# Two output-projection loads a layer: the last two columns moved by 114 and 14 partitions

## The chip, the cores and the metric

The kernel runs on one core of one Trainium2 chip. The metric is device time in microseconds (us) for one execution. Before the change three runs gave 518.45, 520.19 and 518.1 us, median 518.45.

## What is computed

One token passes through two identical layers. Each layer is an attention block A and a mixing MLP block B, both with a residual:

```python
def _A_ref(x, k_cache, v_cache, wq, wo):
    W = min(4096, max(256, Sk // 4))                  # 4096 positions
    q = (x @ wq) per head                             # 32 heads of 192
    k, v = the last W positions of each head's cache
    p = softmax(q k^T * 192 ** -0.5)
    return (p v, all heads side by side) @ wo         # (6144,) @ (6144, 640)

x = x + _A_ref(_layernorm(x), A_k_cache, A_v_cache, A_wq, A_wo)
x = x + _B_ref(_layernorm(x), B_w1, B_w2, B_w3, B_w4)
x = x + _A_ref(_layernorm(x), ...)                    # same weights and caches again
x = x + _B_ref(_layernorm(x), ...)
```

With one position, B's first half falls away (its shifted parts are zero), so B is a layernorm, `w3` (640 x 1536), a gelu and `w4` (1536 x 640). Everything is bf16 in memory. A head's window of K, or of V, is 1.5 MB; they and the weights make the 216 MB that the kernel reads. Layer 1 finds seven transposed K windows and part of the V windows still in SBUF from layer 0.

## The kernel before

**Memory.** One SBUF tensor, `cells`, is cut into eleven cells of 12,288 bytes a partition, each large enough for one head's K or V window. A table, `home`, written out by hand, says which cell each piece uses. `take` claims a cell and `give` frees it in program order; a load into a cell waits until the last reader of the cell's former content is done.

**Loads.** All loads are issued by SP, on one queue, in the fixed order of the list `stream`, and each is called when some later piece of work needs it (`need`). The heads go in groups of four. For each group SP issues K of the next group and V of this one alternately, mostly two heads at a time (`load_both`, line 159: 128 partitions of 24,576 bytes), and then, with one group's delay, the 768 rows of `wo` that belong to the group (`load_wo`, lines 193 to 201: 128 partitions of 7,680 bytes, six rows of `wo` on each partition, "columns" c of 640 values below). Layer 0 takes the groups from the last to the first, layer 1 from the first to the last. So `wo` piece (layer 0, c = 4) is the fourth `wo` load of the kernel, and (0, 2) the sixth; (1, 3) and (1, 5) are the third and fifth of layer 1. The last two `wo` loads of layer 1 are already cut into (3, 3) and (3, 2, 1) columns. At a layer's end come `w3` (`load_w3`, lines 209 and 211) and `w4` (`load_w4`, lines 224 to 229).

**Semaphores.** Each transfer tells of its landing on one of eight semaphores, taken in turn; a transfer whose semaphore was used before waits on SP until the transfer eight places earlier has landed.

**Work on the data.** DVE transposes each K quarter (line 422), PE computes scores (line 501), the softmax steps go over DVE, ACT and PE (lines 530 to 598), PE multiplies with V (line 630), and the group's result is folded (`o_fold`) and multiplied with `wo`: in `out_row` (line 679) for the middle groups and `out_proj` (line 661) or line 701 for the others. `out_row` for a group runs while the next group's softmax is under way. The mixer multiplies with `w3` at line 990 and with `w4` at line 1037, each after the landing of its last piece; layer 1 of attention needs the mixer's result.

The first transfers are five loads of `wq` and, behind the first of them, `load_x` (line 146), which fills five partitions of 256 bytes. At the end the result leaves in the same form from line 1061.

Of the kernel before, what the change touches and what calls it, by code (L numbers as in the profile page):

```python
# [16 lines left out]
P = 128  # L17
# [17 lines left out]
def kernel(  # L35
# [14 lines left out]
    nc = tc.nc  # L50
    _, _, D = A_x.shape
# [22 lines left out]
    NA = Dh // 32  # L74
    NKX = 6
    NKEEP, NCELL = 7, 11
    WARM = 4

# [54 lines left out]
    def take(key):  # L135
        i = cell_of[key] = home[key]
        free.remove(i)
        return cell(i)
# [54 lines left out]
    def load_wo(layer, c):  # L193
        t = take(("wo", layer, c))
        src = A_wo[c * QC:(c + 1) * QC, :].rearrange("(p c) n -> p (c n)", c=NA)
        parts = {NG - 2: (3, 3), NG - 1: (3, 2, 1)}.get(c, (NA,)) if layer == 1 else (NA,)
        i = 0
        for n in parts:
            nc.sync.dma_start(t[:, i * D:(i + n) * D], src[:, i * D:(i + n) * D])
            i += n  # L200
        return t

# [12 lines left out]
    def load_w4(layer):  # L215
# [17 lines left out]
        return blocks  # L233

    LOADERS = {"x": load_x, "k": load_k, "v": load_v, "wq": load_wq, "wo": load_wo, "w3": load_w3, "w4": load_w4}

    def layer_stream(layer):
# [115 lines left out]
    warm_ps = psm.tile([32, 32], F32, tag="psm")  # L353
    for i in range(WARM):
        nc.tensor.matmul(warm_ps[:], lhsT=Eq[:, 0, :], rhs=Eq[:, 0, :], start=(i == 0), stop=(i == WARM - 1))

# [735 lines left out]
```

## Time and profile before

| quantity | value |
|---|---|
| median of three runs | 518.45 us |
| the profiled execution's own time | 518.16 us |
| its span, first to last instruction | 516.4 us |
| read from memory | 216.47 MB, 419 GB/s over the span |
| packets of SP's queue (q1) | 17,572, with 98.6% of the time of 16 DMA engines |
| busy: PE, DVE, ACT | 62%, 55%, 9% of the span |
| `wo` loads of 960 KB | 13, median 28.2 us from issue to landing |

The shares of busy time are averages over the whole span. The DMA share counts the time that packets took on the 16 DMA engines of the core. The trace also keeps a record of each packet (its start, length, size and queue, but not its engine) and of each landing: a 128-partition transfer adds one to its semaphore sixteen times, once for each engine that carried a part of it, and has landed with the sixteenth.

### The profile page before, as it was taken

What the parts mean: (1) busy time and instruction counts of PE and PEld (TensorE: products, weight loads), DVE (VectorE), ACT (ScalarE), POOL (GpSimd) and SP (SyncE); (2) the same over time, 40 slices, a digit from 0 to 9 for tenths busy, and PEclk for the clock granted to TensorE, in tenths of its full rate; (3) what the DMA queues carried; (4) which work ended last, traced back from release to release, by engine and by line L of the source; (5) the groups of instructions that cost most, each with busy time, mean ns of one, the idle gap of its engine ahead of it and who ended that gap; (6) DMA issues with size and microseconds to landing.
All of it is one profiled execution on the core that took longest, in us unless ns stands there. A gap on an engine that the chain in (4) does not pass through costs nothing. (4 is left out here: it accounts for less than half of the span.)

```text
span 516.4 us, 9514 instructions
## 1 busy us (share of the span) xinstructions
PE 318.0 (62%) x4132; PEld 197.3 (38%) x4132; DVE 285.2 (55%) x642; ACT 48.6 (9%) x173; POOL 4.0 (1%) x16
## 2 busy tenths in 40 slices
PE   1046775745386666867645975767474674546775
PEld 0024343423244333544423643444243352323444
DVE  2056668647456565665714256766555764635722
ACT  1000102010010101010101011010010100100011
POOL 2000000000000000000000000000000000000000
PEclk9999998777756567675655588675758677865665
DMA  8999999999999999999999999999999999999995
GB/s 343 438 436 428 429 430 428 435 430 421 440 430 433 428 428 438 420 424 429 428 424 394 384 427 425 441 426 435 428 426 436 428 435 430 425 435 434 424 411 232
DMA packets 17613, 217.07 MB, mean 420 GB/s; under 512 B 1828, under 2 KB 2340, under 8 KB 7972
## 3 DMA queue, kind: packets, MB, share of 16 engines
q1 hardware_dynamic: 17572, 216.48, 98.6%
q8 instruction: 32, 0.52, 0.4%
q14 instruction: 9, 0.07, 0.0%
HBM read 216.47 MB, written 0.00 MB: 419 GB/s over the span
## 5 line engine op out<-in xcount | busy, mean ns | idle before, releaser
L422 DVE STREAM_TRANSPOSE cells<-cells 128x768 uint32<-128x768 uint32 x228 | 203.6, 945 | 43.4 <-DMA cells<-in_A_k_cache_dram 43.1
L501 PE MATMUL ST_ps<-cells,Qblk 128*32 128x256 bf16 x1536 | 157.6, 381 | 108.2 <-DVE cells L422 52.9
L501 PEld LDWEIGHTS <-Qblk 128*32 128x32 bf16 x1536 | 92.2, 125 | 166.9 <-issue 145.6
L630 PE MATMUL O_ps<-cells,PT 128*4 128x384 bf16 x1018 | 96.8, 447 | 9.5 <-DMA cells<-in_A_v_cache_dram 9.2
L639 DVE STREAM_TRANSPOSE o_sb<-O_ps 128x384 f32<-128x384 f32 x32 | 18.6, 583 | 75.7 <-PE O_ps L630 75.7
L630 PEld LDWEIGHTS <-PT 128*4 128x4 bf16 x1024 | 45.4, 102 | 24.9 <-issue 14.1
L653 ACT ACTIVATE oT<-oT_ps,rl 64x6 bf16<-64x6 f32 x32 | 8.3, 260 | 236.7 <-PE oT_ps L650 133.1
L571 DVE STREAM_TRANSPOSE o_sb<-o_sb 128x256 bf16<-128x256 bf16 x14 | 6.2, 445 | 33.1 <-ACT o_sb L566 33.1
L583 PE MATMUL PT_ps<-o_sb,Eq 128*32 128x64 bf16 x224 | 9.6, 292 | 10.1 <-DVE Xq L466 3.4
L583 PEld LDWEIGHTS <-Eq 128*32 128x32 bf16 x256 | 7.4, 112 | 20.8 <-issue 20.7
L452 PE MATMUL qT_ps<-xc,wq_sb 128*128 128x1 bf16 x210 | 7.1, 165 | 13.1 <-DMA wq_sb<-in_A_wq_dram 12.2
L561 ACT COPY nb_sb<-nb_ps 128x2 f32<-128x2 f32 x16 | 2.6, 160 | 124.7 <-PE nb_ps L558 124.7
L441 PE MATMUL qr_ps<-wq_sb,xc 128*1 128x384 bf16 x90 | 13.5, 452 | 0.0
L558 PEld LDWEIGHTS nb_ps<-one,o_sb 1*128 1x128 f32 x56 | 10.4, 252 | 7.4 <-issue 4.3
L566 ACT ACTIVATE o_sb<-ST_ps,nb_sb,sc 128x128 bf16<-128x128 f32 x28 | 13.1, 491 | 0.5
L650 PE MATMUL oT_ps<-o_sb,Lq 128*32 128x6 f32 x160 | 7.3, 191 | 9.4 <-DVE o_sb L639 9.4
L558 PE MATMUL nb_ps<-one,o_sb 1*128 1x1 f32 x56 | 11.7, 302 | 2.0 <-DVE ngm L546 2.0
L679 PE MATMUL yr_ps<-cells,oT 128*1 128x320 bf16 x108 | 12.9, 394 | 0.0
L466 DVE TENSOR_TENSOR Xq<-qT_ps,maskq 128x24 bf16<-128x24 f32 (+1 forms) x18 | 2.8, 155 | 18.1 <-PE qT_ps L452 18.1
L589 PE MATMUL l_ps<-lh,one 128*128 128x4 f32 x32 | 8.5, 335 | 6.6 <-ACT PT L586 6.4
L452 PEld LDWEIGHTS <-wq_sb 128*128 128x128 bf16 x210 | 6.7, 102 | 14.5 <-DMA wq_sb<-in_A_wq_dram 13.3
L650 PEld LDWEIGHTS oT_ps<-o_sb,Lq 128*32 128x32 f32 x160 | 6.1, 131 | 14.8 <-DVE o_sb L639 14.1
(162 smaller groups left out, 204.1 us busy)
## 6 DMA issues: line engine op xcount, KB each, us to landing
cells<-in_A_k_cache_dram SPq DMA_DIRECT2D x23, 3072.0 KB, 19.2
cells<-in_A_v_cache_dram SPq DMA_DIRECT2D x22, 3072.0 KB, 21.7
cells<-in_A_v_cache_dram SPq DMA_DIRECT2D x12, 1536.0 KB, 13.0
cells<-in_A_k_cache_dram SPq DMA_DIRECT2D x11, 1536.0 KB, 14.5
cells<-in_A_wo_dram SPq DMA_DIRECT2D x13, 960.0 KB, 28.2
wq_sb<-in_A_wq_dram SPq DMA_DIRECT2D x5, 1536.0 KB, 13.9
cells<-in_A_v_cache_dram SPq DMA_DIRECT2D x6, 768.0 KB, 15.3
cells<-in_A_v_cache_dram SPq DMA_DIRECT2D x2, 1248.0 KB, 9.3
```

The costliest lines, as they stand in the source:

```text
L422: nc.vector.transpose(Tu, Ku[:, :, q * NY:(q + 1) * NY])
L441: nc.tensor.matmul(qr_ps[32 * i:32 * i + 1, :], lhsT=xc[:, kc:kc + 1], rhs=wq_sb[:, kc, t0 * P + i * N:t0 * P + (i + 1) * N], start=(kc == ...
L452: nc.tensor.matmul(qT_ps[:, tl:tl + 1], lhsT=wq_sb[:, kc, t * P:(t + 1) * P], rhs=xc[:, kc:kc + 1], start=(kc == 0), stop=(kc == ND - 1))
L501: nc.tensor.matmul(ST_ps[r:r + QW, :].rearrange("p (g i) -> p g i", g=ng), lhsT=Q[:, n, :], rhs=T4[:, :, f, :, t], start=(hq == 0 and n == ...
L558: nc.tensor.matmul(nb_ps[:, e:e + 1], lhsT=held["w"][:, e * P:(e + 1) * P], rhs=one[0:1, 0:1], start=True, stop=True)
L566: nc.scalar.activation(out=by_head(Pr)[:, e], in_=by_head(ST_ps)[:, e], func=ACTF.Exp, bias=nb_sb[:, e:e + 1], scale=sc[:, 0:1], accum_out ...
L583: nc.tensor.matmul(PT_ps[32 * m:32 * (m + 1), :, :, ng * q:ng * (q + 1)], lhsT=Eq[:, q, :], rhs=src[:, m:QW:NM], start=True, stop=True)
L589: nc.tensor.matmul(l_ps[:], lhsT=ones, rhs=held["lh"][:], start=True, stop=True)
L630: nc.tensor.matmul(O_ps[r:r + 4, :], lhsT=PT[:, hq, 2 * i:2 * i + 2].rearrange("p c e -> p (c e)"), rhs=v_pair(V, h, 2 * i * Dh, 2 * Dh), ...
L639: nc.vector.transpose(o_sb[:], O_ps.rearrange("p (e a c) -> p e c a", e=2, c=NA))
L650: nc.tensor.matmul(oT_ps[r0 + 32 * n:r0 + 32 * (n + 1), :], lhsT=Lq[:], rhs=o, start=(e == 0), stop=(e == len(terms) - 1))
L679: nc.tensor.matmul(yr_ps[32 * i:32 * i + 1, :], lhsT=oT[:, k:k + 1], rhs=wo_t[:, k * D + i * N:k * D + (i + 1) * N], start=(k == 0), stop= ...
```

## The change

`load_wo` treats four pieces, (0, 4), (0, 2), (1, 3) and (1, 5), in another way. Their first four columns go in one transfer of 128 partitions of 5,120 bytes. The last two columns, 2,560 bytes a partition, go in two transfers: one of partitions 0 to 113, one of partitions 114 to 127.

```diff
+    NEAR = 6 * 19
...
         parts = {NG - 2: (3, 3), NG - 1: (3, 2, 1)}.get(c, (NA,)) if layer == 1 else (NA,)
+        cut = NEAR if (layer, c) in ((0, 4), (0, 2), (1, 3), (1, 5)) else P
+        if cut < P:
+            parts = (NA - 2, 2)
         i = 0
         for n in parts:
-            nc.sync.dma_start(t[:, i * D:(i + n) * D], src[:, i * D:(i + n) * D])
+            for r in (slice(0, cut), slice(cut, P)) if i and cut < P else (slice(0, P),):
+                nc.sync.dma_start(t[r, i * D:(i + n) * D], src[r, i * D:(i + n) * D])
             i += n
```

SP issues 8 more transfers in all. The bytes, the cells, the order of all other transfers and the instructions of PE, DVE, ACT and POOL are as before.

## The prediction

> **What bounds the kernel.** I read first the page's slices and queues, then the chain of waits, then SP's timeline around the four changed loads and around the layer boundary.
>
> ```profile
> span 516.4 us, 9514 instructions
> ...
> DMA  8999999999999999999999999999999999999995
> ...
> q1 hardware_dynamic: 17572, 216.48, 98.6%
> q8 instruction: 32, 0.52, 0.4%
> q14 instruction: 9, 0.07, 0.0%
> ...
> 413.84 18.21 DMA cells<-in_A_k_cache_dram
> 444.87 19.43 DMA cells<-in_A_k_cache_dram
> 483.11 18.83 DMA cells<-in_A_wo_dram
> 502.01 10.45 DMA cells<-in_B_w_dram
> 512.51 0.84 PE y_ps L1037 x25
> ...
> 133.99 0.69 SPq L199 DMA_DIRECT2D cells<-in_A_wo_dram  x1
> 152.30 0.54 SPq L159 DMA_DIRECT2D cells<-in_A_k_cache_dram  x1
> 208.99 0.33 SPq L199 DMA_DIRECT2D cells<-in_A_wo_dram  x1
> 213.25 0.54 SPq L164 DMA_DIRECT2D cells<-in_A_k_cache_dram  x1
> 276.94 0.42 SPq L229 DMA_DIRECT2D cells<-in_B_w_dram  x1
> 281.93 4.66 SPq L178 DMA_DIRECT2D cells<-in_A_v_cache_dram  x2
> 289.92 3.98 SPq L164 DMA_DIRECT2D cells<-in_A_k_cache_dram  x2
> ```
>
> The DMA engines are busy in every slice, and the chain (start, length, what) goes from landing to landing until 512.46, when w4's last pair lands; what follows is 3.9 us. So the kernel ends when the latest DMA engine ends, and the question is which engine that is.
>
> **Lanes.** In the packet records, while a queue is full, a packet starts 3 ns before the one ahead of it on its engine ends, and all engines go through the same sequence of sizes. With that the packets can be strung into sixteen lanes. A 128-partition transfer puts eight rows on each lane, and the lanes keep their distances to within some 10 ns for long stretches. Only instruction fetches shift them. A q8 fetch (16 KB) puts its lane back by 1.41 us, and the 32 of them go round eight lanes ("fetch lanes"). A q14 fetch (8 KB) costs 0.55 to 0.85 us, and three of them in each layer (at 55, 134, 226 and at 315, 396, 498) fall on one other lane, the "heavy" one. The seven others are "quiet". Lateness behind the earliest lane at the last w4 load of each layer, in us:
>
> ```
> layer, earliest end   fetch lanes                              heavy  quiet lanes
> 0, 282.2   2.67 3.00 3.15 2.87 1.93 3.16 3.12 3.19    2.43   0.55 0.36 0.01 0.00 0.24 0.23 0.49
> 1, 509.3   2.47 2.16 2.28 1.90 2.35 3.23 2.33 2.29    2.63   0.25 0.00 0.00 0.04 0.09 0.75 1.12
> ```
>
> The load of x, five rows, ran as five packets on five lanes: the heavy one and the first four quiet ones of layer 0's row.
>
> **Part 1: who carries what.** The two shapes in the trace are split into equal numbers of whole rows (16 x 8, 5 x 1). The most engines that can share 114 rows equally are 6, with 19 rows each; 14 rows go on 14. I take it that a transfer on few engines starts from the same engine each time, so the six include x's five, the heavy lane among them. [...]
>
> **Part 2: price of a split.** Medians of the packet records: 2,560 bytes 102 ns, 4,608 bytes 178, 6,144 bytes 234, 7,680 bytes 291; between 178 and 234, 5,120 bytes come to 197. A lane's step is 3 ns less, and 6 for the landing note. Before: 8 x 288 + 6 = 2,310 ns on each lane. After: 8 x 194 + 6 = 1,558 on all; plus 19 x 99 + 6 = 1,887 on six; plus 99 + 6 on fourteen. The six carry 3,550 (+1.24 us), eight others 1,663 (-0.65), two 1,558 (-0.75). Two splits a layer: +2.48, -1.29, -1.50. The 102 ns is for rows that each lane writes to its own partitions. A transfer spread like this one isn't in the trace; the ends are 99 ns a step and, if two lanes writing into one group of partitions halve each other's rate, 198. I take 99: x's five 256-byte packets, also outside the usual sharing out, took 18 ns each, and the sizes above extrapolate to 17.
>
> **Part 3: layer 0.** The heavy lane ends at 2.43 + 2.48 = 4.91 after 282.2, where the latest was at 3.19: +1.72 us. The fetch lanes fall to 1.90 at most, which nobody waits for. A quiet lane of the six comes to 3.03. The last w4 piece is what layer 0's last five matmuls (285.73) wait for, so layer 1's first scores and SP's issue at 289.92, which wait for them, shift by 1.72.
>
> **Part 4: the boundary.** Before, the heavy lane needed 17.63 us of packets (four loads of 3.66 and one of 2.98) between its end of w4 (284.63) and 303.78, so it lost 1.52 there to late issues and slow first packets. After, it comes to the 289.92 issue (then 291.63, its packets free to start 2.3 later as in the trace) at 287.11 + 2 x 3.66 = 294.43, half a microsecond after they can start, and may lose less. Its shift into layer 1 is 0.94 to 1.72.
>
> **Part 5: layer 1.** No lane starves from 300 us on. The heavy lane ended at 509.3 + 2.63 = 511.93. Now: + 0.94 to 1.72 + 2.48 = 515.35 to 516.13. The latest lane before ended at 512.53. So + 2.8 to 3.6 us; I take 3.5, since slow first packets follow any late issue.
>
> **Part 6: SP, semaphores, readers, at nothing.** Eight more issues of 0.33 to 0.7 us each. Behind the first two stand the K loads above, 18 and 4 us later and waiting for cells; behind the other two 17 us. Each split moves the transfer that semaphore reuse waits for two places later: the tightest is the K load issued at 226.81, which would wait for the first four columns of (0, 2), landing at about 227, and whose packets start only at 238. The readers of the four pieces run at 178.8, 229.6, 408.7 and 472; the second has the least room, as its piece landed at 227.55 and comes some 1.7 us later.
>
> **Sum.** The profiled execution took 518.16, 0.29 under the median. 518.16 + 3.5 = 521.7; beside the median, 522.0 (own range 521.2 to 522.8).
>
> **Rivals.** *Shared partition groups* (32 in 100): the six lanes write 114 partitions, most of which other lanes are filling with the next K load at the same time. If a row then takes twice as long, 19 x 99 = 1.88 us more a split, 3.76 a layer: 1.72 + 3.76 + 1.88 + 3.76 = 11.1, so 529.6; if half of the rows meet another lane, 525.8. For it: a lane's rate of 24,576 bytes in 909 ns leaves no sign of a reserve. Against: x's 18 ns, though 256 bytes is little. [...]
>
> *The heavy lane isn't among the six, or its q14 fetches fall elsewhere in this build* (22 in 100). Then the six quiet lanes take the slack that they have: layer 0 ends with the latest at 0.55 + 2.48 = 3.03 in place of 3.19 (-0.16), layer 1 with 1.12 + 2.48 = 3.60 or 0.75 + 2.48 = 3.23 in place of 3.23: 518.3 to 518.7, not slower by anything that can be told. It decides as long as the latest of the six would end a layer less than about 0.75 behind the earliest lane, for 0.75 + 2.48 is the old 3.23. For it: which engine a fetch queue uses isn't in the program. Against: x's packets lie on the heavy lane, which its lateness of 0.26 at the first load tells from its neighbours at 0.22 and 0.30.
>
> *A real gain* (5 in 100): with all lanes level, each layer would end at the mean lateness, 1.70 and 1.49, which is 1.49 and 1.74 under the latest, so 515.2 is the floor. Lanes moved by 2.48 and -1.29 can come near it only if the fetches are spread otherwise in this build. *Fewer engines* (5 in 100): 114 rows on two engines, 57 x 99 = 5.6 us a split, over 530.
>
> **Chances.** The forecast has 36 in 100. Range 517.8 to 529.6: no change, the forecast and the sharing of ports. What a measurement here can tell is about 0.5%, 2.6 us. Slower by more: forecast, sharing, fewer engines, 0.73; within: the third case and a little of the others, 0.22; faster 0.05.
>
> **What would show it.** In the profile after: q1 has 4 x 128 = 512 more data packets; at the end of each layer the sixteen landings of a transfer are spread over about 5 us in place of 3.2, with one lane last by over 1 us; the landings of w4 come 1.7 us later in layer 0 and 3.5 in layer 1. [...] If the spread stays at 3 us, the heavy lane isn't in the six and I am wrong.

## The result and the profile after

The changed kernel takes 531.99 us (median of six, 529.44 to 538.17), the kernel before 519.17 beside it. The run of 538.17 fell in a slow state and is left out of the ratio, which is 1.0243, 95% interval 1.0224 to 1.0262: 12.6 us slower. The profiled execution took 531.84 us. The forecast was 522.0 and the range ended at 529.6: the direction was right, the size was not.

Lines of the page of the changed kernel:

```profile
span 530.1 us, 9524 instructions
...
DMA  8999999999999999999999999999999999999895
...
q1 hardware_dynamic: 18164, 216.48, 98.1%
...
cells<-in_A_wo_dram SPq DMA_DIRECT2D x4, 640.0 KB, 31.8
```

The bytes are the same, there are 592 more packets (512 of data, 80 landing notes), and the span is 13.7 us longer at nearly the same share, 98.1% where it was 98.6%. In time, the packets took 10.6 us more on each of the sixteen engines, and the engines were without a packet for 3.1 us more. So for the most part they did not wait for the program; they took longer for the same bytes. The four 640 KB transfers are the four-column parts.

The end of the chain of waits (start, length, what):

```profile
512.46 2.73 PE O_ps L635 x16
515.36 10.43 DMA cells<-in_B_w_dram
525.84 0.84 PE y_ps L1042 x25
```

It still ends with the landing of w4's last pair, which is now at 525.79 where it was at 512.46: 13.3 us later; only 0.4 us more is lost behind it. Around the first two splits, the view by stretches (stretch, its length, busy time and count of PE, PEld, DVE, ACT and POOL, granted clock, DMA share, GB/s), first before, then after:

```profile
160.00:164.00 4.00, 3.72 (x50) 2.39 (x46) 4.00 (x6) 0.26 (x1) 0.00 (x0) 0.50 1.06 453
164.00:168.00 4.00, 1.88 (x33) 1.24 (x31) 0.99 (x3) 0.26 (x1) 0.00 (x0) 0.93 0.96 410
224.00:228.00 4.00, 2.63 (x45) 1.49 (x38) 2.16 (x5) 0.20 (x1) 0.00 (x0) 1.00 1.00 422
228.00:232.00 4.00, 2.42 (x52) 1.99 (x50) 1.87 (x9) 1.21 (x6) 0.00 (x0) 0.68 1.02 427
```

```profile
160.00:164.00 4.00, 3.62 (x47) 2.02 (x50) 3.38 (x4) 0.26 (x1) 0.00 (x0) 0.50 1.08 311
164.00:168.00 4.00, 1.96 (x36) 1.10 (x25) 0.75 (x2) 0.26 (x1) 0.00 (x0) 0.85 1.00 377
224.00:228.00 4.00, 1.84 (x17) 1.02 (x18) 3.56 (x4) 0.00 (x0) 0.00 (x0) 0.83 1.05 366
228.00:232.00 4.00, 2.95 (x37) 1.79 (x32) 1.17 (x4) 0.26 (x1) 0.00 (x0) 0.75 1.00 292
```

The DMA share stays near 1 while the rate falls to 292 to 377 GB/s: the same engines, full, move less. The packet records say which packets are longer. In the four splits 378 of the 512 rows of 2,560 bytes took longer than the 102 ns of elsewhere; the means of the splits are 141 to 150 ns and most of the long ones lie between 115 and 200. Of the 512 rows of 5,120 bytes, 166 were longer than their 196 ns, up to 374. Behind the first, third and fourth split the 24,576-byte rows of the K load took up to 1,593 ns (912 elsewhere), and behind the second, where loads of 12,288 bytes a partition follow, those rows took up to 826 (460). So not only the six lanes that carry the 114 rows are slow, but also the lanes that have gone on to the next load. Adding up what packets took beyond their usual length and dividing by sixteen gives 1.8, 2.4, 2.0 and 2.2 us for the four splits, 8.4 in all. This sum is called the *excess* below. (The other 2 us of longer packets lie outside the splits, between 240 and 310 us and after 490 us.) The uneven load that the prediction worked out is 4 x 1.24 = 5.0 more; 13.4 together, where the end moved by 13.3. That the two numbers meet so closely is partly luck: the excess is a mean over sixteen lanes, and the end is set by one.

### The profile page after: what moved, and what is told of

The parts are those of the page before. It is cut to its first block, busy times and chain, and to the rows that moved or that the text cites. A ratio compares the mean times of both kernels' runs of the same rounds, so it can differ in the third digit from the quotient of the medians.

```text
span 530.1 us, 9524 instructions
## 1 busy us (share of the span) xinstructions
PE 311.3 (59%) x4132; PEld 193.7 (37%) x4132; DVE 284.9 (54%) x642; ACT 48.3 (9%) x173; POOL 4.0 (1%) x16
## 3 DMA queue, kind: packets, MB, share of 16 engines
q1 hardware_dynamic: 18164, 216.48, 98.1%
## 5 line engine op out<-in xcount | busy, mean ns | idle before, releaser
L506 PE MATMUL ST_ps<-cells,Qblk 128*32 128x256 bf16 x1536 | 151.2, 369 | 121.8 <-DVE pm L535 61.2
L506 PEld LDWEIGHTS <-Qblk 128*32 128x32 bf16 x1536 | 89.9, 122 | 177.9 <-issue 159.0
L635 PE MATMUL O_ps<-cells,PT 128*4 128x384 bf16 x1018 | 95.3, 452 | 13.5 <-DMA cells<-in_A_v_cache_dram 13.0
L635 PEld LDWEIGHTS <-PT 128*4 128x4 bf16 x1024 | 44.0, 103 | 31.5 <-issue 20.2
L457 PE MATMUL qT_ps<-xc,wq_sb 128*128 128x1 bf16 x210 | 7.1, 165 | 13.4 <-DMA wq_sb<-in_A_wq_dram 12.5
L591 ACT CAST PT<-PT_ps 128x256 bf16<-128x256 f32 x16 | 7.1, 445 | 44.9 <-PE PT_ps L588 44.9
```

The lines of the kernel that those rows point to most:

```text
L457: nc.tensor.matmul(qT_ps[:, tl:tl + 1], lhsT=wq_sb[:, kc, t * P:(t + 1) * P], rhs=xc[:, kc:kc + 1], start=(kc == 0), stop=(kc == ND - 1))
L506: nc.tensor.matmul(ST_ps[r:r + QW, :].rearrange("p (g i) -> p g i", g=ng), lhsT=Q[:, n, :], rhs=T4[:, :, f, :, t], start=(hq == 0 and n == ...
L635: nc.tensor.matmul(O_ps[r:r + 4, :], lhsT=PT[:, hq, 2 * i:2 * i + 2].rearrange("p c e -> p (c e)"), rhs=v_pair(V, h, 2 * i * Dh, 2 * Dh), ...
```

## The experiments

Two theories stood against each other, and a third had to be ruled out. *Shared groups*: a set of partitions takes bytes at one lane's rate; in a transfer of 128 partitions each lane has its own set, and rows cut otherwise put two lanes on one set. *Uneven load*: six lanes carry 1.24 us more a split, and nothing else happens. *More pieces*: transfers and packets cost time by themselves. Each ratio is against the kernel before, run beside it.

| kernel | time, us | ratio, 95% interval |
|---|---|---|
| two transfers of 128 | 519.1 | 1.0008 (0.9998 to 1.0017) |
| three transfers of 128 | 519.83 | 1.0011 (1.0002 to 1.0021) |
| 112 and 16 | 527.55 | 1.0167 (1.0132 to 1.0202) |
| 64 and 64 | 526.42 | 1.0147 (1.013 to 1.0164) |
| 108 and 20 | 526.78 | 1.0151 (1.0136 to 1.0166) |
| 114 and 14, the change | 531.99 | 1.0243 (1.0224 to 1.0262) |
| 115 and 13 | 531.05 | 1.0227 (1.021 to 1.0244) |
| 114 and 14, (1, 3) alone | 521.13 | 1.0056 (1.0043 to 1.0069) |
| 114 and 14, one column | 524.07 | 1.0103 (1.0053 to 1.0154) |
| even and odd partitions | 544.76 | 1.0509 (1.0493 to 1.0526) |
| before + six rows, memory to memory | 522.57 | 1.0082 (1.0069 to 1.0095) |
| 112 and 16 + these six rows | 527.0 | 1.0179 (1.0125 to 1.0232) |

### Pieces without moved rows

```diff
-        cut = NEAR if (layer, c) in ((0, 4), (0, 2), (1, 3), (1, 5)) else P
-        if cut < P:
+        cut = P
+        if (layer, c) in ((0, 4), (0, 2), (1, 3), (1, 5)):
             parts = (NA - 2, 2)
```

> The four pieces are cut into columns 0 to 3 and 4 to 5 as in the change, but both transfers have all 128 partitions; the cut into 114 and 14 is gone. Shared groups (a partition group takes bytes at one lane's rate, and rows that another lane normally fills make two lanes share a group): no row is moved to another lane, so 518 to 520 us and ratio 0.997 to 1.003, 2,560-byte packets at 102 ns, 5,120 at 196. Uneven load alone (six lanes carry more, nothing is shared): the same, since the load is even. More and smaller pieces (transfers and packets themselves cost the time): it keeps four of the eight added transfers and all 512 added packets, so at least half of the 12.8 us, 525 or more.

The second form has `parts = (NA - 2, 1, 1)`.

> Each of the four pieces in three transfers of all 128 partitions, of four columns, one and one: as many transfers as in the changed kernel, and 1,024 added packets in place of 512, all on the lanes that normally fill these partitions. Shared groups: 518.3 to 520, ratio 0.999 to 1.003. If the number of transfers or of packets costs the time: 526 or more.

The first can't be told from no change. The second, with as many transfers as the changed kernel and twice its added packets, costs 0.1 to 1.1 us of the 12.6. So transfers, packets, SP's issues and the reuse of semaphores are not the cause.

### An even cut that moves rows to other lanes

```diff
-    NEAR = 6 * 19
+    NEAR = 112
```

> The split is 112 and 16 partitions in place of 114 and 14: seven rows and one row on each of sixteen lanes, so every lane carries the same eight rows, but most rows lie on partitions that another lane normally fills. Shared groups: the lengthening stays without the imbalance; the excess packet time of the changed kernel's trace, 8.4 us averaged over the lanes, stays whole or in part: 523 to 528, 2,560-byte packets 130 to 200 ns. Uneven load alone: 518 to 520, packets at 102 ns. More pieces: as the changed kernel, 530 or more.

With `NEAR = 64`:

> The split is 64 and 64 partitions: four rows and four rows on each lane, even load. Shared groups: all sixteen lanes write first into one half of the partitions and then into the other, so if a group takes one lane's rate, each of the two transfers runs at half rate, about 0.4 us a transfer or 3 us in all by itself, and more where the next load's lanes wait for it: 521 to 528, with 2,560-byte packets near 200 ns. Uneven load alone: 518 to 520, 102 ns. More pieces: 530 or more.

Both are slower, by 8.7 and 7.6 us going by their ratios, though every lane carries eight rows as before (each has 18,212 packets on q1, 640 more than before: 512 of data and 128 landing notes, which is sixteen for either part of a cut). Uneven load alone is out as the main cause. The stretches of 112 and 16 show the dip of the changed kernel:

```profile
160.00:164.00 4.00, 3.54 (x66) 2.19 (x64) 2.98 (x4) 0.26 (x1) 0.00 (x0) 0.83 1.11 338
164.00:168.00 4.00, 0.77 (x13) 0.26 (x7) 0.75 (x2) 0.26 (x1) 0.00 (x0) 1.00 1.00 422
224.00:228.00 4.00, 2.79 (x40) 1.45 (x38) 2.41 (x3) 0.00 (x0) 0.00 (x0) 1.00 1.06 327
228.00:232.00 4.00, 2.23 (x44) 1.82 (x45) 1.81 (x8) 1.30 (x6) 0.00 (x0) 1.00 0.99 355
```

The excess is 6.6 us here and 6.8 with 64 and 64. That 64 and 64 costs as much as 112 and 16 answers the expectation's "3 us by itself": the lengthening of the cut rows themselves is the smaller part (their mean is 130 to 143 ns in place of 102, which is 0.2 to 0.3 us of the 1.2 to 2.0 of a split); the rest is lost by the four-column rows ahead of them and, for the greater part, by the rows of the load behind.

### The transfers by themselves

> A measurement of the transfers by themselves; it leaves out the whole computation and returns x. Six stretches run a load of 128 x 12,288 bytes, then 128 x 2,560 bytes whole or cut at 114, 112, 64 or 120, then 128 x 24,576 bytes; after that, with nothing else under way, loads of 12,288 bytes a partition into 128 partitions, into 16 neighbouring ones, into 16 at steps of 4 and of 8, into the first 32, the first 64, every second, the first 112 and the first 114. Shared groups: packets of 460 ns where every lane has its own group; longer by a whole factor with fewer groups than lanes, alone too: 16 neighbouring partitions the longest (two times or more), 64 partitions about 920 ns; and in the stretches the 114 and 112 cuts lengthen the packets of the test and of the load behind it (over 950 ns for 24,576 bytes), the whole one doesn't. Uneven load alone and more pieces: 460 ns alone for any set of partitions, 102 and 912 ns in all stretches.

The stretches took 12.87 us whole (13.16 the first time), 15.11 with 114 and 14, 13.62 with 112 and 16, 13.49 with 64 and 64, 13.79 with 120 and 8. Alone, packets of 12,288 bytes had a median of 460 ns into 128 partitions, 713 into the first 32, 887 into the first 64, 460 into every second partition and 687 into the first 112. The two sets of 64 have the same source rows, of two heads, and differ otherwise only in where they go; so it is the target that is shared. The first 114 had 460 as well: six lanes alone hardly meet, and the cut shows its price beside other loads. The three sets of 16 put one packet on each lane, the slow first one (488 to 939), and tell nothing. So they were run with more transfers one behind the other:

> A measurement of the transfers by themselves; it leaves out the whole computation and returns x. Stretches of three to seven loads of 12,288 bytes a partition, one behind the other, into: all 128 partitions, 0 to 15, 0 to 60 at steps of 4, 0 to 120 at steps of 8, 0 to 31, 0 to 63, 0 to 126 at steps of 2, 0 to 30 at steps of 2, 64 to 79. Sixteen groups made of eight neighbouring partitions: packets of 460 ns times 16 lanes over the groups that the set has: 460, 3,680, 920, 460, 1,840, 920, 460, 1,840, 3,680. Sixteen groups of four neighbours and the four that lie 32 above them: 460, 1,840, 920, 920, 920, 920, 460, 920, 1,840. No groups (a lane's own rate is all there is): 460 for every set.

| partitions | median ns a packet | if groups are eight neighbours | if four and the four 32 above |
|---|---|---|---|
| 0 to 127 | 460 | 460 | 460 |
| 0 to 15 | 1,805 | 3,680 | 1,840 |
| 0 to 60, steps of 4 | 957 | 920 | 920 |
| 0 to 120, steps of 8 | 965 | 460 | 920 |
| 0 to 31 | 961 | 1,840 | 920 |
| 0 to 63 | 958 | 920 | 920 |
| 0 to 126, steps of 2 | 460 | 460 | 460 |
| 0 to 30, steps of 2 | 951 | 1,840 | 920 |
| 64 to 79 | 1,805 | 3,680 | 1,840 |

The view by stretches, inside the first, second, sixth and last of these sets (stretch, its length, DVE and POOL, clock, DMA share, GB/s):

```profile
4.00:13.00 9.00, 0.00 (x0) 0.00 (x0) 1.00 1.02 436
18.00:26.00 8.00, 0.00 (x0) 0.00 (x0) 1.00 1.12 120
...
69.00:84.00 15.00, 0.00 (x0) 0.00 (x0) 1.00 1.00 205
...
114.00:122.00 8.00, 0.00 (x0) 0.00 (x0) 1.00 1.11 118
```

All sixteen lanes work in each, and the rate goes with the number of groups: 436 GB/s with sixteen, 205 with eight, and with four about 109 by the packets (sixteen of 12,288 bytes in 1,805 ns; the 118 and 120 of the view count packets by their start, which its shares of 1.11 and 1.12 show). With groups of four neighbours and the four that lie 32 above them, 460 ns times the lanes on a group comes to within 5% of every row; with eight neighbours five of the nine are off by a factor of 1.9 or more. The grouping is known here from these nine sets alone.

### In the stream: same rows, same lanes' load, other targets

> A measurement of the transfers by themselves; it leaves out the whole computation and returns x. Fifteen stretches, drained in between: a load of 128 x 12,288 bytes, the test, a load of 128 x 24,576 bytes, each in a tile of its own. The test is 2,560 bytes a partition, five forms three times over: whole; 0 to 113 and 114 to 127; 0 to 63 and 64 to 127; even and odd partitions; 32 to 95, 0 to 31 and 96 to 127. Shared groups (four neighbouring partitions and the four that lie 32 above them): whole 12.9 us; 114 and 14 some 2.2 longer; halves 0.6 longer with packets over 102 and 912 ns; even and odd not longer than whole (within 0.2), with packets of 102 and 912, since every group is filled by one lane; the middle 64 undisturbed and the two quarters disturbed, 0.2 to 0.5 longer. If any second transfer of 64 rows costs time by itself, even and odd cost as much as the halves.

| form, three times each | stretch, us | mean ns of 2,560 bytes | of 24,576 bytes behind it |
|---|---|---|---|
| whole | 13.37 (the first), 12.92, 12.85 | 102 | 912 |
| 114 and 14 | 15.01, 15.08, 16.27 | 149, 151, 158 | 1,024, 1,028, 1,053 |
| 64 and 64 | 13.77, 13.72, 13.68 | 139, 139, 144 | 970, 974, 965 |
| even and odd | 12.94, 12.91, 13.02 | 102 | 912, 912, 915 |
| middle 64 and two quarters | 13.39, 13.40, 13.57 | 112, 110, 116 | 961, 950, 961 |

The second round of five, stretch by stretch:

```profile
79.64:92.56 12.92, 0.00 (x0) 0.00 (x0) 1.00 0.96 390
94.41:109.50 15.09, 0.00 (x0) 0.00 (x0) 1.00 0.93 334
111.45:125.17 13.72, 0.00 (x0) 0.00 (x0) 1.00 0.94 367
127.14:140.05 12.91, 0.00 (x0) 0.00 (x0) 1.00 0.95 391
141.88:155.28 13.40, 0.00 (x0) 0.00 (x0) 1.00 0.95 377
```

Two transfers of 64 rows cost nothing that shows (within 0.2 us) when they are the even and the odd partitions, and 0.8 us when they are the lower and the upper half. Same transfers, bytes and rows a lane; only the groups differ. The middle 64 and two quarters cost 0.5 to 0.7 us. With 114 and 14 the stretch is 2.1, 2.2 and 3.4 us longer, of which 1.24 is uneven load by the prediction's working.

The stretches show the cause, but not all of its size: four times 0.8 us is 3.2, and 64 and 64 cost 7.6 in the kernel, where the excess of its four splits is 1.2, 1.8, 1.8 and 2.0 us. In a stretch the same adding up gives 0.8. A stretch starts with nothing under way, and the landings of its first load lie 0.8 us apart (the first stretch with halves); in the kernel the lanes are further apart, with the sixteen landings of an earlier load spread over 2.1 to 3.4 us. That this makes the difference was not tried apart.

In the kernel the even and odd cut could not show this (`cut` is now only true or false, for the same four pieces):

```diff
...
-            for r in (slice(0, cut), slice(cut, P)) if i and cut < P else (slice(0, P),):
+            for r in (slice(0, P, 2), slice(1, P, 2)) if i and cut else (slice(0, P),):
```

> The last two columns of the four pieces go in two transfers of 64 partitions, the even ones and the odd ones, in place of the first and the last 64: the same transfers, packets, bytes and load of the lanes, but each lane's rows stay on the eight partitions that it normally fills. Shared groups: no lengthening, 518 to 520, ratio 0.997 to 1.003, packets at 102, 196 and 912 ns. If any second transfer of 64 rows costs this time (pieces, order on the queue): 525 to 527, as with the first and the last 64.

It took 26 us more. SP's timeline (start, length, line, how many):

```profile
134.25 0.54 SPq L159 DMA_DIRECT2D cells<-in_A_v_cache_dram  x1
134.83 30.52 SPq L203 DMA_DIRECT2D cells<-in_A_wo_dram  x3
165.44 0.55 SPq L159 DMA_DIRECT2D cells<-in_A_k_cache_dram  x1
```

SP stands at the first stepped transfer from 135 until 164.22, which is after everything issued before it has landed (162.48), and the queue runs empty. SP's table of waits names the K transposes, which read other cells:

```profile
SPq L203 <- DVE cells L426: 106.1, 6, 29.8
```

The four-column part, which goes into the same cell, was issued without such a wait; so the stepped rows brought waits for cells that they don't touch. This run therefore says nothing of the groups, and the even and odd cut is shown in the stretches alone.

### The uneven load, and what it adds

The kernel before, with rows that load six lanes and go to no partition; their data is used by nothing (this edit is against the kernel before):

```diff
             i += n
+        if (layer, c) in ((0, 4), (0, 2), (1, 3), (1, 5)):
+            dummy = nc.dram_tensor(f"dummy{layer}{c}", (6, 16640), BF16, kind="Internal").ap()
+            nc.sync.dma_start(dummy, A_v_cache[0, c, 0:1024, :].rearrange("(p j) d -> p (j d)", p=8)[0:6, 0:16640])
         return t
```

> The kernel before, with one added transfer behind each of the four pieces: six rows of 33,280 bytes from memory to memory, one on each of six lanes (1.24 us each if a lane takes them at the rate of 24,576 bytes in 912 ns; more if memory as a target is slower). Its data is used by nothing. It puts extra load on six lanes without touching SBUF. Uneven load: the end moves by the added time of one lane, four times, less the slack that the heaviest of the six has: 3 to 5 us if the packets take 1.24, 522 to 524. Shared groups: it adds nothing to that, as the packets of the other loads keep 912 ns. If the six lanes have slack for it, 519.

Each of the 24 rows took 1,232 ns, the packets beside them kept their lengths (the stretches below are close to those of before), and the end moved by 4.2 us: w4's landing by 1.97 in layer 0 and 4.22 in layer 1.

```profile
160.00:164.00 4.00, 3.54 (x66) 2.20 (x64) 2.99 (x4) 0.26 (x1) 0.00 (x0) 0.84 1.08 457
164.00:168.00 4.00, 0.78 (x13) 0.27 (x7) 0.76 (x2) 0.26 (x1) 0.00 (x0) 1.00 0.95 406
224.00:228.00 4.00, 2.62 (x39) 1.64 (x38) 2.41 (x5) 0.00 (x0) 0.00 (x0) 1.00 1.06 448
```

So uneven load alone costs a little more than the prediction gave it (1.72 and 3.5). Does it come on top? First the same rows behind the even cut:

> The even split of 112 and 16 partitions (8.7 us by itself) and behind each of its four pieces the six rows of 33,280 bytes from memory to memory (4.2 us by itself). If the changed kernel's time is the sum of shared groups and uneven load, the two together give it back: 518.9 + 8.7 + 4.2 = 531.8, 530 to 534. If one hides in the other (the extra load of six lanes fits into the time that shared groups cost), 528 or less.

Not in full: 527.0, where the sum was 531.8. The intervals are wide, 6.5 to 12.0 us with the rows and 6.9 to 10.5 without, so a part of the 4.2 may come on top. In the profiled executions it does: w4's last landing is 4.3 us late in layer 0 and 9.3 in layer 1, against 2.9 and 7.5 with the even cut alone, while the excess is 4.8 us in place of 6.6. Then the cut was moved, so that other numbers of rows go to the busiest lanes. `NEAR = 5 * 23`, and `NEAR = 12 * 9`:

> 115 and 13 partitions: 23 rows on each of five lanes, then one on each of thirteen, so five lanes carry 24 rows (16 x 99 ns = 1.58 us more than eight rows a split, against 1.24 on six lanes with 114 and 14). If the extra rows of the few lanes come on top of what shared groups cost (7.5 to 8.7 us with an even load): 519 + 8 + 4 x 1.58 = 533, 531 to 536, slower than the changed kernel or equal. If the extra load hides in the shared groups' time, as with the memory-to-memory rows: 526 to 529.

> 108 and 20 partitions: nine rows on each of twelve lanes, two on each of ten, so ten lanes carry eleven rows (3 x 99 ns = 0.30 us more a split), two carry nine and four none. On top: 519 + 8 + 4 x 0.30 = 528, 526.5 to 529.5. If the size of the first transfer alone set the time (fewer rows on the first one, less time): near 64 and 64 or 112 and 16, whichever lane carries what.

115 and 13 is no slower than the change; 108 and 20 is like the even cuts. The few-lane cuts thus cost about 4 us more than the even ones, the size that six loaded lanes cost alone, but not in proportion to the extra rows. Added up as for the changed kernel, excess and extra rows of the most loaded lanes come to within 1 us of the delay of w4's last landing in each of these kernels: 6.6 beside 7.5 (112 and 16), 6.8 beside 7.0 (64 and 64), 4.8 + 4.9 beside 9.3 (112 and 16 with the six rows), 7.6 + 6.3 beside 13.4 (115 and 13), 7.2 + 1.2 beside 8.6 (108 and 20). So once the packets' own lengths are counted the uneven load does come on top; what can't be told ahead is the excess, which was 1.8 us smaller with the six rows. That 115 and 13 is no slower has a further reason that fits the lanes' lateness, though it was only worked out: if with 115 the five lanes are those that carried x, the heavy one and four quiet ones, the heavy lane ends layer 0 at 2.43 + 2 x 1.58 = 5.6. With 114 the sixth lane is a fetch lane (its fetches lie at 42 and 188 us in the changed kernel's trace), and a fetch lane at up to 3.19 ends at 3.19 + 2 x 1.24 = 5.7.

### One split, and half the bytes

With only `(1, 3)` in the list:

> Only the piece (1, 3) is split, the other three are whole. Shared groups with uneven load: one split of four, in the layer that ends last; in the changed kernel this one gave 2.0 us of excess packet time and its imbalance is 1.24, so 3.2 us, 521.0 to 522.6, ratio 1.004 to 1.008. If the splits were worse than additive (each loses more because the lanes are already apart), less than 2 us.

With `parts = (NA - 1, 1)`, so that 1,280 bytes a partition are cut:

> 114 and 14 partitions as in the change, but for the last column alone (1,280 bytes a partition). Shared groups with uneven load: both parts go with the bytes; by the packets' lengths (55 ns against 102) 0.54 of 12.8 us, so 524 to 526.5, ratio 1.011 to 1.016. If a split costs a fixed time, whatever it carries: 529 or more.

One split costs 2.9 us (2.2 to 3.6), a quarter of the whole within its interval. Half the bytes cost 5.3 us by the ratio, but with an interval of 2.8 to 8.0; w4's last landing is 5.5 us late in the profiled execution, where 13.3 was that of the whole. So most of the price goes with the bytes; a small fixed part is not ruled out.

## Why the prediction missed

**Part 1, who carries what: right.** That a transfer on few engines starts from the same engine each time was assumed, and no row before showed 114 rows. In the trace after, the 114 rows have six landing notes and the 14 have fourteen (the 80 more are 4 x (16 + 6 + 14 - 16)), with the heavy lane among the six: after the first split four of the six land at 163.1 to 163.5 us and two at 165.6 and 166.4. The sixth lane, which the prediction left unnamed, is by the lanes strung from the packets a fetch lane, as late as the heavy one.

**Part 2, the price of a split: the step that failed.** It took 99 ns for a row of the 114, from x's five packets and between ends of 99 and 198. Measured, such rows took 141 to 150 ns on the mean in the kernel's splits and 149 to 158 in the stream, and the step gave nothing at all to the lanes that are met. The row it was judged by was the wrong one: x's packets have 256 bytes and took 18 ns, and no row showed that they met another packet. The row nearest in kind was a lane's own 24,576 bytes in 909 ns, which the text itself read as "no sign of a reserve": if a group is filled at a lane's full rate by its own lane, a second lane can't be free.

**The rival with shared groups: right in kind, still short.** Its "twice as long" was an assumption, as no row before had two lanes on one group; the sets gave 951 to 965 ns for 460 with two lanes on each group, the kernel's splits 141 to 150 for 102. Its 525.8 to 529.6 priced the rows of the six lanes only. It left out that the lane which is met loses as well: the 24,576-byte rows behind the cut went from 912 to about 1,030 ns on the mean in the stream. The excess falls on all lanes: after the first split the earliest landing of the next K load comes 1.3 us later and the latest 2.7. It deserved the larger chance, and with this term the sum 8.4 + 5.0 would have been 531.9 beside the median of 518.45; but 8.4 is known only from the trace after.

**Parts 3 and 5, the uneven load: right as a term, a little small.** 1.72 in layer 0 and 3.5 in all (2.8 to 3.6) were forecast; the six loaded lanes gave 1.97 and 4.2. In the changed kernel w4's landing moved by 6.2 and 13.3, because the other term was missing.

**Part 4, the boundary: nothing came back.** Forecast was that 0.94 to 1.72 of 1.72 is carried over. The last landings are 6.2 us late at 285.68 and 6.2 at 383.2. With the six loaded lanes alone they are 1.97 late at the first place and 2.8 at the second, so the boundary added where the working had it give back. SP's issues shifted with the mixer, as the working had it:

```profile
282.80 1.25 SPq L234 DMA_DIRECT2D cells<-in_B_w_dram  x1
287.92 4.85 SPq L179 DMA_DIRECT2D cells<-in_A_v_cache_dram  x2
296.10 3.49 SPq L165 DMA_DIRECT2D cells<-in_A_k_cache_dram  x2
```

The issue at 296.10 was at 289.92 before.

**Part 6, at nothing: right.** The twofold and threefold transfers of 128 partitions cost 0.1% (at most 0.2%).

**The other rivals** are out: the heavy lane is among the six, the 114 rows went over six engines and not two, and nothing was gained. The spread of the sixteen landings, offered as a sign of the heavy lane, reached 7.5 us after the second split and 7.8 after the fourth; at the layers' ends the early lanes ran out of work and it fell to 4.0 and 3.4. (In layer 1 the first landing of one load came at 491.58, and SP issued the next only at 493.20.) What decided was the length of the 2,560-byte packets inside the splits, 141 to 150 ns on the mean, where the median before was 102.

**Open:** what sets the size of the excess. With 64 and 64 it is 1.2 to 2.0 us a split in the kernel and 0.8 in the stretches, and memory-to-memory rows behind the even cut make it smaller. That the six lanes, while away from SBUF, leave room for the others fits this, but was not tried apart. No version here beats the kernel before: the bytes that each group must take don't change with the lane that brings them.

## What to carry to other kernels

Where transfers are the bound, count the partition groups that each one covers at a time, not only its lanes and bytes: a cut along partitions that is balanced in rows can still be slow (1.5 to 1.7% here), while a cut along the free dimension cost at most 0.2%. Price a disturbance on both sides, the lane that comes and the lane that is met. And when an unknown price lies between "free" and "twice", ask first whether the shared thing already runs at its full rate.

## What the runs showed of the hardware

- With groups counted as four partitions and the four 32 above, the count that fits all nine sets, one lane to a group ran at 27 GB/s (24,576 bytes in 909 ns); two lanes on each group made packets of 460 ns 951 to 965, four lanes 1,805, so that the group took no more.
- The lanes that are met slow down too: packets of 24,576 bytes that followed a cut took up to 1,593 ns (912), and the rate over 4 us fell from 427 to 292 GB/s.
- Rows from memory to memory ran at 33,280 bytes in 1,232 ns on their lane, as fast as loads into SBUF (27 GB/s), and lengthened no packet beside them.
- 128 rows landed in sixteen parts, 114 in six, 14 in fourteen, and the five rows of x were five packets.
